# RWKV-7 attention and a GELU MLP on one core: the state turned in 64x64 tiles, fewer columns in the last chunk, and a new order of steps

## The chip, the cores and the metric

The kernel runs on one core of a Trainium2 chip (trn2). The metric is the time of one execution in microseconds of the device. Before the change it is the median of three runs.

## What is computed

Two blocks follow each other. The first is the recurrence of RWKV-7 over 768 time steps, for 4 x 8 heads of 40 x 40 state. The second takes the 3072 rows of 320 numbers that come out, and applies an MLP with an exact GELU.

```python
batch, n_heads, seq, head_dim = (4, 8, 768, 40)
n_tokens, d_model, d_ff = (3072, 320, 2048)
...
for t in range(S):
    kt, vt, rt = (k[:, :, t], v[:, :, t], r[:, :, t])
    wt, at, bt = (w[:, :, t], a[:, :, t], b[:, :, t])
    y[:, :, t] = np.einsum('bhd,bhde->bhe', rt, state)
    Sa = np.einsum('bhde,bhe->bhd', state, at)
    state_decay = state * wt[:, :, None, :] - np.einsum('bhd,bhe->bhde', Sa, bt)
    state = state_decay + np.einsum('bhd,bhe->bhde', vt, kt)
...
x = np.ascontiguousarray(attn_out.transpose(0, 2, 1, 3)).reshape(B * S, H * D)
h = x @ w_in
g = 0.5 * h * (1.0 + erf(h * inv_sqrt2))
return (g @ w_out).astype(np.float32)
```

Note that the state after the last time step is returned to nobody.

## The kernel before

**Chunks.** Time is cut into 12 chunks of C = 64 steps. Inside a chunk the recurrence is solved with matrix products: four products between the 64 steps (N, A, RV and the read of the old state), the inverse of a triangular matrix per head, and sums with the values. From chunk to chunk only the state goes on. All 32 heads are worked on together, two batches (e) by two (g), eight heads as four pairs (i) by two (x). A tile of partitions holds 64 rows of one half and 64 of the other, so most products are small: 40 or 64 rows by 64 columns, and matmuls on the four quadrants of the array follow each other. One fp32 matmul stands as two instructions in the trace.

**Combined columns.** VC = 104 columns are moved together where it goes: the first D = 40 belong to the next state, the other C = 64 to the outputs of this chunk. VR holds v beside the masked product RV, SM the solved right sides, st the state (40) beside the product of r with the state (64).

**The steps of a chunk c, and where they stand.** They are generators under `@step`; each `yield` ends one piece.

- `N` (t["nT"], t["aT"] to N): product on PE, mask on DVE, two stores to DRAM. `nb` loads that back with another layout, `inv` solves it on POOL in four pieces and stores it, `ft` loads the inverse into Tt. `corner` (L922 the transpose on DVE, then PE, then a copy on ACT to Js, L930) and `joined` (PE, and copies on ACT and DVE, L945) complete it.
- `A` and `RV` (masks at L692), `av` (A times VR, into PSUM), `X` (adds a times the state; two copies on ACT to SM at L957), `sa` (Tt times SM; two masks on DVE, L981).
- `tn` turns the state: a product with the identity on PE, and a copy on ACT into `turned` (L993). `yy` reads it: r times the state, into the 64 right columns of st (L1017).
- `QY` and `qk` (by_rows) sum SM and VR with b and k into PSUM; in the last chunk they move only the right 64 columns already. Then `state` makes the new state (L1098 to L1101) and `y` the outputs (L1048, L1049), which SP moves into xt.
- The MLP of the chunk: `ph` is the first matrix (chunks below 3 whole, L1175; from 3 on a scheme with seven products per half, L1200 and L1207, with copies `pc` on ACT at L1238, additions `pd` on DVE at L1244 and GELUs `pg` on ACT at L1250), `po` the second (L1272, then seven products at L1288), `tx` sums of x on DVE. Between ph's fifth and sixth product a copy (pc) and an addition (pd) read what the sixth goes on adding to.
- `co` and `ci` turn the weights, which arrive as pairs of words, into floats on DVE and ACT (L472 to L488). `warm` is a dummy product of 512 columns into a PSUM buffer that nobody reads.

Small steps load and scale: `a`, `b`, `k`, `v`, `r`, `w`, `wq`, `vp`, `bp`, `kp` issue loads on SP; `ta`, `tb`, `tk`, `tv`, `tr`, `wt` turn them on DVE (L577); `sk` (L621) scales on POOL; `sums` are the decay sums on PE with an Exp on ACT.

**The order** is written out by hand as one long list, ORDER. Each token takes a step one `yield` on, so the list is the program order of all five engines and of SP's queue, and each engine runs its own part of it in that order, waiting where data or a buffer isn't ready. Numbers behind colons name buffers: one of four PSUM buffers `duo0` to `duo3`, each two banks wide, or one of three `conv` tiles in SBUF. PSUM is only these four buffers, so a step must also wait until its buffer's last reader is done.

```python
for token in ORDER.split():
    name, *at = token.strip("*").split(":")
    places[:] = [int(x) for x in at]
    if name not in going:
        kind = name.rstrip("0123456789")
        going[name] = steps[kind](int(name[len(kind):]))
    next(going[name], None)
```

Constants of this case: NT = NB = NW = 3 and NS = 2 are the chunks up to which loads, turns and products have their first form, NP = 4 pairs of heads, G = 2, BW = 80, TW = 640. A matmul is recorded at L154 (`mm`), except those of ph, po and the transposes.

Of the kernel before, what the change touches and what calls it, by code (L numbers as in the profile page):

```python
# [35 lines left out]
sa0:0 sa0 sa0:1 tk1 warm3:2 wi0 wo0 inv1 sa0 tr1:0 QY0:1:2 wi0 qk0 ci9:0 logs2 tv1 ci3:1 ci9 tr1 ci9 y0 wl0 wl0 inv1
b2 state0 co0:0 sums2:0 co1:2 ci3 ci3 a2 wi1 sums2:3 sums2 r2 tn1:1 r2 wi1 wi1 sc2 A1:2 A1 co0 y0:3 ci4:1 tables0
sums2 y0:0 y0 y0 RV1:2 wi1 wi1 RV1 ci4 inv1 tn1 tr2:0 tr2 ta2:1 co0 co1 tb2:2 ta2 av1:0:3 tb2 zeros8 yy1:1 wo2 yy1 ci4
ci6:0 yy1 ci6 k2 ci7:1 inv1 co1 inv2 wi1 v2 ci6 ci8:2 ph0:2 X1 N2:1 sk2 X1 ph0 ft1 N2 ci8 corner1:0 X1 ph0 ph0:0
corner1:3 ci8 ph0 ci7 wo4 ft1 zeros6 tk2:2 zeros7 corner1 co3:0 co3 co5:2 co5 co3 wo9 zeros5 ft1 ci7 tv2:3 co2:0 N2 N2  # L40
a3 a3 joined1:1 ph0 ph0:0 wo8 co2 ph0 co9:1 tv2 co2 co4:0 joined1 joined1 co4 co9 co4 nb2 co9 tk2 co5 sa1:1:3 RV2:2
wo6 w3 inv2 sa1 nb2 ph0 ph0:0 ph0 co8:2 kp3 ph0 co6:1 sa1 w3 co7:0 wq3 co7 wo15 wq3 QY1:3:1 kp3 RV2 ta3 bp3 qk1 po0:2
po0 wo13 co6 co6 y1 bp3 co7 wt3:1 A2:0 state1 po0 y1 y1 y1 wt3 vp3 tn2:1 A2 av2:0:3 tn2 co8 logs3 wt3 wo10 yy2:1 yy2
vp3 vp3 po0 y1 co8 yy2 b3 co13:2 wt3 tb3 sums3:1 sums3 X2 wo12 ph1:1 co11:1 a4 co10:0 co10 co11 co11 vp3 X2 wo14 ta3
# [53 lines left out]
def kernel(  # L98
# [1300 lines left out]
```

## Time and profile before

| what | value |
|---|---|
| median of three runs | 658.70 us (658.08 to 658.98) |
| profiled execution | 657.67 us |
| its span, first to last instruction | 656.0 us |
| mean granted TensorE clock | 0.995 |
| moved by DMA | 80.73 MB, mean 123 GB/s |

The profiled execution is one run of its own, so a sum of parts is made against 657.67 us and its span, and the median is what a change is measured by. A row of the timeline gives start and length in us, engine, line, operation, what is written and read with buffer numbers left out, the shape and the number of instructions that were merged, and in brackets the idle time ahead with what ended it. Matmuls overlap at their ends, so the time of a step on TensorE is read from its start to the start of the next one.

### The profile page before, as it was taken

Reading aid. Unit: us, or ns where it says so; the run is one execution under the profiler, and the core shown is the slowest. Engines: PE = TensorE matmul, PEld = TensorE weight load, DVE = VectorE, ACT = ScalarE, POOL = GpSimd, SP = SyncE. Lnnn points to the kernel's source line nnn. Section 1 sums busy time; section 2 is a strip of 40 time slices with the busy share of each in tenths; the row PEclk is TensorE's granted clock in tenths of the full one; section 3 lists DMA queues with packets and bytes.
Section 4 is the critical chain, followed back from the end, with each engine's and each line's share of the span. In section 5 each row is a group of like instructions: output and inputs, shape, how many; then the busy total and the mean of one; then the engine's idle time right before and its main releaser. Section 6 shows DMA issues by size and latency. Waiting matters only on the chain.

```text
span 656.0 us, 30927 instructions
## 1 busy us (share of the span) xinstructions
PE 636.9 (97%) x13840; PEld 578.9 (88%) x13840; DVE 479.1 (73%) x643; ACT 272.4 (42%) x326; POOL 384.7 (59%) x797
## 2 busy tenths in 40 slices
PE   9998899999999999999999999999999999999987
PEld 5986788778788999999989999999999998999987
DVE  1698999998756986877886968967869854727332
ACT  4366362642253335337245346335346344134130
POOL 5258708826868838818848828848838848800000
PEclk9999999999999999999999999999999998999989
DMA  9989999687676585975696686775886673230100
GB/s 130 168 164 189 189 209 173 147 138 144 128 135 131 102 160 102 154 140 109 131 155 121 123 152 123 122 137 115 160 143 120 131 118 63 53 66 16 39 2 20
DMA packets 298949, 80.73 MB, mean 123 GB/s; under 512 B 287656, under 2 KB 292400, under 8 KB 298816
## 3 DMA queue, kind: packets, MB, share of 16 engines
q1 hardware_dynamic: 297952, 76.40, 63.3%
q0 software_dynamic: 864, 2.36, 2.3%
q8 instruction: 108, 1.77, 1.2%
q14 instruction: 25, 0.20, 0.1%
HBM read 65.40 MB, written 11.01 MB: 116 GB/s over the span
## 4 chain that ended last, share of the span: by engine, by line
PE 58%; DVE 14%; SPq 9%; DMA 7%; POOL 5%; issue 4%; ACT 2%; DVEq 0%; POOLq 0%; ACTq 0%
PE duo L1288 18%; PE duo L154 15%; PE duo L1200 15%; SPq L222 9%; PE duo L1207 4%; PE duo L1175 3%; PE duo L1272 3%; POOL os L817 2%; POOL rows L815 2%; DVE st L1101 1%; DMA Tt<-inv 1%; DVE xt L1049 1%; DVE conv L577 1%; DVE xt L1048 1%; DMA r_pairs<-in_r_dram 1%
## 5 line engine op out<-in xcount | busy, mean ns | idle before, releaser
L815 POOL TENSOR_TENSOR tmp<-W,Nb 128x56 f32<-128x56 f32 (+22 forms) x155 | 75.7, 489 | 48.0 <-DMA Nb<-N 36.2
L815 POOL TENSOR_TENSOR tmp<-rT,Nb 128x56 f32<-128x56 f32 (+22 forms) x155 | 73.1, 471 | 43.7 <-DMA Nb<-N 32.0
L1288 PE MATMUL duo<-w_out_sb,gt 128*128 128x160 f32 x640 | 92.5, 302 | 0.2 <-DVE gt L1314 0.2
L1288 PEld LDWEIGHTS duo<-w_out_sb,gt 128*128 128x128 f32 x640 | 87.7, 190 | 2.2 <-issue 0.4
L817 POOL TENSOR_TENSOR W<-W,tmp 128x56 f32<-128x56 f32 (+22 forms) x155 | 77.6, 500 | 12.2
L817 POOL TENSOR_TENSOR rT<-rT,tmp 128x56 f32<-128x56 f32 (+22 forms) x155 | 71.6, 462 | 12.2
L1200 PE MATMUL duo<-xt,w_in_sb 64*128 64x128 f32 x864 | 62.1, 276 | 0.0
L1238 ACT COPY gt<-duo 128x1024 f32<-128x1024 f32 x27 | 27.3, 1011 | 75.8 <-PE duo L1200 38.9
L1244 DVE TENSOR_TENSOR gt<-gt,duo 128x1024 f32<-128x1024 f32 x27 | 32.8, 1214 | 35.4 <-ACT gt L1238 18.0
L1207 PE MATMUL duo<-xt,w_in_sb 64*128 64x128 f32 x576 | 57.5, 276 | 0.0
L1200 PEld LDWEIGHTS duo<-xt,w_in_sb 64*128 64x128 f32 x864 | 54.2, 188 | 3.7 <-ACT SM L957 1.5
L1175 PE MATMUL duo<-xt,w_in_sb 64*128 64x256 f32 x480 | 54.8, 381 | 0.2 <-ACT w_tile L537 0.2
L1175 PEld LDWEIGHTS duo<-xt,w_in_sb 64*128 64x128 f32 x480 | 45.5, 187 | 5.9 <-ACT w_tile L537 0.4
L1288 PE MATMUL duo<-extra,conv 128*128 128x160 f32 x320 | 45.8, 301 | 1.0 <-DVE conv L1295 0.7
L1207 PEld LDWEIGHTS duo<-xt,w_in_sb 64*128 64x128 f32 x576 | 45.5, 192 | 0.0
L1288 PEld LDWEIGHTS duo<-extra,conv 128*128 128x128 f32 x320 | 43.8, 190 | 1.8 <-DVE conv L1295 0.9
L621 POOL TENSOR_TENSOR rows<-rows,w_tile 128x640 f32<-128x640 f32 x9 | 15.2, 1686 | 49.4 <-ACT w_tile L537 44.3
L957 ACT COPY SM<-duo 128x832 f32<-128x832 f32 x22 | 18.3, 852 | 47.6 <-PE duo L154 42.1
L1272 PE MATMUL duo<-w_out_sb,gt 128*128 128x320 f32 x128 | 36.9, 440 | 0.0
L1292 DVE TENSOR_TENSOR os<-os,duo 128x160 f32<-128x160 f32 x40 | 12.7, 317 | 31.4 <-PE duo L1288 27.2
L1250 ACT ACTIVATE gt<-gt 128x1024 f32<-128x1024 f32 x27 | 27.8, 1053 | 17.5 <-DVE gt L1244 17.4
L1272 PEld LDWEIGHTS duo<-w_out_sb,gt 128*128 128x128 f32 x128 | 23.6, 190 | 9.5
(257 smaller groups left out, 1421.6 us busy)
## 6 DMA issues: line engine op xcount, KB each, us to landing
Nb<-N SPq DMA_DIRECT2D x18, 256.0 KB
VR<-in_v_dram SPq DMA_DIRECT2D x24, 160.0 KB
out_dram<-os SPq DMA_DIRECT2D x48, 80.0 KB
rows<-in_b_dram SPq DMA_DIRECT2D x22, 160.0 KB
rows<-in_k_dram SPq DMA_DIRECT2D x22, 160.0 KB
w_out_sb<-in_moe_w_out_dram SPq DMA_DIRECT2D x5, 640.0 KB
w_tile<-in_w_dram SPq DMA_DIRECT2D x36, 80.0 KB
Tt<-inv SPq DMA_DIRECT2D x44, 64.0 KB
```

What stands on the lines that cost most here:

```text
L154: nc.tensor.matmul(o, lhsT, rhs, start=first, stop=True, skip_group_check=True)
L222: queue[0].dma_start(out=out, in_=in_)
L815: eng.tensor_tensor(t, W[:, :nr, j:j + 1].to_broadcast([P, nr, rest]), Nb[:, j:j + 1, j + 1:].to_broadcast([P, nr, rest]), ALU.mult)
L817: eng.tensor_tensor(W[:, :nr, j + 1:], W[:, :nr, j + 1:], t, ALU.add)
L1175: nc.tensor.matmul(pt[:, x, s], w_in_sb[half(x), kt, p * P:(p + 1) * P], xt[half(x), kt], start=kt == 0, stop=kt == NK - 1)
L1200: nc.tensor.matmul(out_of(pt)[:, x, j], left(kt, j)[half(x)], right[half(x), kt], start=first and j == 0 and kt == 0, stop=True, skip_grou ...
L1207: nc.tensor.matmul(out_of(pt)[:, x, j], w_in_sb[half(x), NP, at:at + P], xt[half(x), NP, cols], start=False, stop=True, skip_group_check=True)
L1238: nc.scalar.copy(block_of(f, g), out_of(of(c)["u"]))
L1244: nc.vector.tensor_tensor(block_of(f, g), block_of(f, g), out_of(of(c)[v_]), ALU.add)
L1250: nc.scalar.activation(block_of(f, g), block_of(f, g), ACT.Gelu)
L1272: nc.tensor.matmul(pt[:, g], gt[:, f, g * P:(g + 1) * P], w_out_sb[:, f], start=f == 0, stop=f == NF - 1)
L1288: nc.tensor.matmul(pt[:, n, :DM // 2], l_[:, f], r_[:, f], start=f == 0, stop=f == NF // 2 - 1)
```

## The change

Three things change. First, `tn` keeps its form for chunks 1 and 2, and from chunk 3 (NB) on it takes the two halves of the rows apart: 32 products of 40 rows and 40 columns on the four quadrants of the array, in place of 16 products of 128 rows and 80 columns; the copy reads PSUM in another pattern. Second, `wanted(c)` is the right 64 columns in the last chunk, and all 104 before; `av`, `X` with its copies and `sa` with its masks use it. So v of the last chunk is loaded but read by nobody. Third, ORDER is another one. It has the same 1553 tokens. Up to the second chunk's QY it is nearly the old sequence, with PSUM buffers 0 and 2 exchanged in the first lines; behind that the tokens stand in another sequence, with other buffers. Among them `warm7` moves from between `corner3` and `joined3` to behind `yy1`, and `warm4` from ahead of `corner7` to between the fifth and the sixth product of `ph11`.

The diff, with ORDER cut to the lines that hold the places the prediction speaks of:

```diff
@@ -29,68 +29,68 @@
...
-r4 po1 ft3 corner3:2 ph2:0 ph2 ft3 corner3:1 ft3 ph2 ww0 tr4 a5 warm7:3 a5 ws3 vp5 vp5 vp5 inv4 vp5 corner3 joined3:0
...
-sums7 sc7 pc6 ph6 po5 inv7 kp8 pc6 N8 ph6:3 ph6 wt9:2 N8 pd6 pg6 ft7 tk8:0 po5:1 ft7 warm4:0 corner7:0 nb8 corner7:0
-pc6 po5 pd6 A8:1 nb8 A8 corner7 ft7 joined7:0 joined7 joined7 ph6 a9 r8 r8 r8 sk7 w8 sa7:0:1 pg6 inv8 r8 ta9 inv8 w8
...
-nb9 nb9 tx7 tx7 inv10 ph7 ph7:1 pc7 ph7 po6:3 ft8 wt10:2 ft8 a10 wt10 pd7 sk8 r9 w9 corner8:0 wt10 pc7 r9 corner8:0
-po6 pd7 A9:3 corner8 inv9 joined8:0 joined8 joined8 inv9 ph7 A9 pd7 sa8:3:0 tx7 pg7 ph7 sa8 r9 pg7 pg7 a10 pg7 vp10
...
-N10:3 po7 a11 a11 sums9:1 y8 N10 tk10:2 inv9 ph8:0 pc8 ph8:3 tx8 ph8 inv9 ph8:2 po7 inv9 inv9 pc8 vp10 tv10 ph8 sums9
-tx8 N10 pd8 N10 ft9 corner9:2 ft9 ta11 nb10 nb10 ft9 po7:1 corner9:3 pg8 pc8 wq11 po7 sc9 pd8 A10:1 A10 wq11 bp11 sk9
...
-QY11:0:1 qk11 pg10 pg10 pd10 y11 y11 y11 pg10 po9 po10:0 pg10 po10:3 y11 po10 y11 po10:2 y11 po10 po10 po10:1 po10
-po10 y11 po10 po10 po10:3 po10 po10 y11 tx11 po10 po10:1 ph11:3 ph11:0 po10 po10 tx11 pc11 tx11 ph11 pc11 pd11 ph11:0
-ph11 pc11 pd11 ph11 pg11 tx11 tx11 ph11 pd11 pg11 pg11 pg11 po11:1 po11:0 po11 po11:2 po11 po11 po11:3 po11 po11 po11
...
+inv3 warm7:0 wo2 tails1 yy1 ci4 ci6:0 yy1 ci6 k2 ci7:1 inv1 co1 inv2 wi1 v2 ci6 ci8:2 ph0:0 X1 N2:2 sk2 X1 ph0 wo8 ft1
...
+ph6:3 po5 N8 wt9 tx6 ph6 ft7 sc7 corner7:0 ft7 corner7:2 tk8:0 ft7 nb8 po5 po5:1 nb8 corner7 joined7:2 joined7 po5
+ph6:1 a9 r8 pc6 pd6 joined7 ta9 pg6 sa7:2:3 sa7 sk7 sa7 ph6 pc6 pd6 QY7:2:3 tx6 tx6 r8 r8 qk7 state7 ph6 pd6 pg6 ph6
...
+sums8 a10 ph7:1 pc7 ph7:2 ph7 ph7:3 vp10 X8 pc7 pd7 corner8:0 corner8:2 corner8 ft8 ph7 A9:2 vp10 wt10 r9 r9 joined8:0
+tx7 sk8 pc7 pd7 A9 inv9 joined8 ph7 tx7 joined8 sa8:0:2 ta10 pd7 r9 r9 sc8 sa8 vp10 w9 sa8 vp10 w9 ph7 inv10 QY8:2:0
...
+X9 tx8 po7 a11 y8 N10 N10 N10 inv9 tv10 A10:2 wq11 tx8 sums9:3 po7 po7:0 sums9 po7 sc9 tx8 nb10 ph8:3 pc8 ph8:0 ta11
+pd8 X9 ph8 pc8 wq11 wt11:2 nb10 tx8 ph8:0 ph8 pc8 ft9 sk9 corner9:0 ft9 ft9 corner9:1 corner9 r10 joined9:1 joined9
+pg8 r10 pd8 ph8 A10 pg8 r10 joined9 tx8 pd8 sa9:1:2 w10 w10 wt11 ph8 bp11 r10 sa9 sa9 QY9:2:1 logs10 wt11 pg8 pg8 tr10
...
+y9 y9 po8:0 po8 y9 y9 sums10 kp11 tn10 sc10 k10 RV10 po8 av10:1:3 yy10:2 vp11 inv10 ta11 po8 po8 tb11 yy10 po8:0 po8
...
+QY11:1:0 k11 sk11 qk11 y11 y11 y11 y11 y11 po10 po10:2 po10 po10 y11 po10:0 po10 po10 tx11 po10 po10 tx11 tx11 po10:2
+po10 y11 po10 po10 po10:0 ph11:2 v11 y11 ph11:1 pc11 ph11 ph11:3 pd11 pc11 pg11 tx11 ph11 tx11 pc11 pd11 warm4:1 ph11
+pg11 ph11 pd11 po10 po10 pg11 po11:1 po11:0 pg11 po11 po11:2 po11 po11 po11:2 po11 po11 po11 po11 po11:0 po11 po11
...
@@ -770,8 +770,12 @@
             return
         t["av"] = [duo()[:, :, :NP * VC].rearrange("p g (i d) -> p g i d", i=NP) for x in range(2)]
         for g, i, x, e, q, m in units(True):
-            mm(t["av"][x][half(e ^ x), g, i], t["A"][half(e), x, g, i], VRs[c % 2][half(e), g, q, m], i == 0)
-        yield
+            mm(t["av"][x][half(e ^ x), g, i, wanted(c)], t["A"][half(e), x, g, i], VRs[c % 2][half(e), g, q, m, wanted(c)],
+               i == 0)
+        yield
+
+    def wanted(c):
+        return slice(D if c == NCH - 1 else 0, VC)
 
     sm_of = SM.rearrange("p g q (a x) c -> p x g (q a) c", x=2)
 
@@ -951,10 +955,11 @@
     def X(c):
         t = of(c)
         for g, i, x, e, q, m in units():
-            mm(t["av"][x][half(e ^ x), g, i], t["aT"][half(x, D), g, i, e], st[half(x, D), e, i, g], False)
+            mm(t["av"][x][half(e ^ x), g, i, wanted(c)], t["aT"][half(x, D), g, i, e], st[half(x, D), e, i, g, wanted(c)],
+               False)
         yield
         for x in range(2):
-            nc.scalar.copy(sm_of[:, x], t["av"][x])
+            nc.scalar.copy(sm_of[:, x, :, :, wanted(c)], t["av"][x][:, :, :, wanted(c)])
             yield
 
     @step
@@ -975,22 +980,33 @@
             return
         pt = [duo()[:, :, :NP * VC].rearrange("p g (i d) -> p g i d", i=NP) for x in range(2)]
         for g, i, x, e, q, m in units():
-            mm(pt[x][half(e), g, i], Tt_tile[half(e ^ x), x, g, i], sm_of[half(e ^ x), x, g, i])
+            mm(pt[x][half(e), g, i, wanted(c)], Tt_tile[half(e ^ x), x, g, i], sm_of[half(e ^ x), x, g, i, wanted(c)])
         yield
         for x in range(2):
-            nc.vector.tensor_tensor(sm_of[:, x], pt[x], left_upper.unsqueeze(1).unsqueeze(1).to_broadcast([P, G, NP, VC]),
-                                    ALU.mult)
+            mask = left_upper.unsqueeze(1).unsqueeze(1).to_broadcast([P, G, NP, VC])[:, :, :, wanted(c)]
+            nc.vector.tensor_tensor(sm_of[:, x, :, :, wanted(c)], pt[x][:, :, :, wanted(c)], mask, ALU.mult)
             yield
 
     @step
     def tn(c):
-        pt = duo()[:, :, :NP * BW].rearrange("p e (n t) -> p e n t", n=NP)
+        if c < NB:
+            pt = duo()[:, :, :NP * BW].rearrange("p e (n t) -> p e n t", n=NP)
+            for e in range(2):
+                for i in range(NP):
+                    for g in range(G):
+                        mm(pt[half(g), e, i], st[:, e, i, g, :HP], ident.rearrange("p (x d) -> p x d", x=2)[:, :, :D])
+            yield
+            nc.scalar.copy(turned[:, :TW].rearrange("p (e n) -> p e n", e=2), pt.rearrange("p e n t -> p e (n t)"))
+            yield
+            return
+        pt = duo()[:, :, :G * NP * D].rearrange("p x (n d) -> p x n d", d=D)
         for e in range(2):
             for i in range(NP):
                 for g in range(G):
-                    mm(pt[half(g), e, i], st[:, e, i, g, :HP], ident.rearrange("p (x d) -> p x d", x=2)[:, :, :D])
-        yield
-        nc.scalar.copy(turned[:, :TW].rearrange("p (e n) -> p e n", e=2), pt.rearrange("p e n t -> p e (n t)"))
+                    for x in range(2):
+                        mm(pt[half(g), x, e * NP + i], st[half(x, D), e, i, g, :HP], ident[half(x, D), half(x, D)])
+        yield
+        nc.scalar.copy(turned[:, :TW].rearrange("p (n x d) -> p x n d", x=2, d=D), pt)
         yield
 
     def sums_of_y(c):
```

More of the change, by code (lines that the diff above doesn't have):

```diff
@@ L41 @@
[L41 to L44, printed above, removed]
-co13 ph1 ph1 ph1:0 co10 ph1 inv2 ph1 ph1:1 tv3 co13 co14:0 co15:2 a4 co14 inv2 inv2 k3 inv2 co15 co12:1 ph1 X2 co14
@@ L94 @@
+joined11:0 sums11 sc11 ph10 tx10 joined11 ph10 pd10 po9 joined11 sa11:0:1 pg10 sa11 sa11 pg10 pg10 po10:0 pg10 po10:2
+QY11:1:0 k11 sk11 qk11 y11 y11 y11 y11 y11 po10 po10:2 po10 po10 y11 po10:0 po10 po10 tx11 po10 po10 tx11 tx11 po10:2
+po10 y11 po10 po10 po10:0 ph11:2 v11 y11 ph11:1 pc11 ph11 ph11:3 pd11 pc11 pg11 tx11 ph11 tx11 pc11 pd11 warm4:1 ph11
+pg11 ph11 pd11 po10 po10 pg11 po11:1 po11:0 pg11 po11 po11:2 po11 po11 po11:2 po11 po11 po11 po11 po11:0 po11 po11
+po11 po11:2 po11 po11
 """
```

95 lines of the change are left out of this document (48 added, 47 removed).

## The prediction

> **What bounds the kernel now.** I read the page first, then the busy time by stage, then the waits, then the timeline. The page gives the shares.
>
> ```profile
> span 656.0 us, 30927 instructions
> ...
> PE 636.9 (97%) x13840; PEld 578.9 (88%) x13840; DVE 479.1 (73%) x643; ACT 272.4 (42%) x326; POOL 384.7 (59%) x797
> ```
>
> TensorE is busy for 97% of the span. A share is a mean over stages, so the stages come next (start:end, length, then busy time of PE, PEld, DVE, ACT, POOL, granted clock, DMA share, GB/s).
>
> ```profile
> 72.00:148.00 76.00, 73.23 (x1439) 60.49 (x1438) 72.68 (x126) 36.47 (x48) 40.33 (x86) 1.00 0.85 170
> 148.00:240.00 92.00, 91.48 (x1883) 77.65 (x1874) 70.26 (x81) 33.92 (x40) 66.28 (x135) 1.00 0.70 132
> 240.00:540.00 300.00, 297.77 (x7069) 283.34 (x7069) 233.14 (x281) 133.21 (x151) 204.69 (x410) 1.00 0.73 131
> 540.00:656.00 116.00, 107.40 (x1972) 103.94 (x1964) 52.68 (x76) 31.80 (x39) 30.93 (x64) 0.97 0.19 38
> ```
>
> From 148 to 540 us TensorE idles 0.5 + 2.2 us of 392, so an instruction taken from it there shortens the run, as long as no wait takes its place. Before 148 VectorE is as full (72.68 of 76). After 540 there are 8.6 idle us, and the clock falls to 0.97. The waits name the causes (total, times, longest).
>
> ```profile
> PE duo L154 <- issue: 4.5, 4, 1.7
> PE duo L1200 <- DVE gt L1244: 2.6, 2, 2.4
> ...
> PE duo L154 <- DVE conv L922: 0.7, 1, 0.7
> ...
> DVE conv L922 <- DMA Tt<-inv: 12.6, 5, 5.3
> ```
>
> The 2.4 us wait is ph's sixth product, which stands behind an addition on VectorE. In the last row VectorE waits for the inverse that came back through memory, five times: that chain arrives just in time, though TensorE pays only 0.7 us for it yet (the row above).
>
> **The change part by part.** *The turned state.* tn has 16 matmuls of 128 rows, 64 weight columns and 80 moving columns, which the trace records as 32 instructions. From chunk 3 on it is 32 matmuls of 40 rows and 40 moving columns, 64 instructions, nine times. The new form is in no row, so it is bounded by its neighbours. The timeline of chunk 11 (start, length):
>
> ```profile
> 569.80 1.33 PE L154 MATMUL duo<-ident,st 128*64 128x80 f32 x32
> 571.05 1.66 PE L154 MATMUL duo<-VR,nT 64*64 64x104 f32 x64
> 572.53 1.11 PE L154 MATMUL duo<-rT,turned 40*64 40x64 f32 x64
> 573.57 2.44 PE L1288 MATMUL duo<-extra,gt 128*128 128x160 f32 x16
> 575.94 1.66 PE L154 MATMUL duo<-st,aT 40*64 40x104 f32 x64
> 577.53 2.50 PE L1200 MATMUL duo<-xt,w_in_sb 64*128 64x128 f32 x40
> ...
> 593.77 1.66 PE L154 MATMUL duo<-SM,Tt 64*64 64x104 f32 x64
> 595.35 0.71 PE L1200 MATMUL duo<-xt,w_in_sb 64*128 64x128 f32 x8
> ...
> 598.23 1.16 PE L154 MATMUL duo<-SM,rows 64*64 64x64 f32 x64
> 599.22 1.11 PE L154 MATMUL duo<-VR,rows 64*64 64x64 f32 x64
> 600.26 4.61 PE L1288 MATMUL duo<-w_out_sb,gt 128*128 128x160 f32 x32
> ```
>
> A step costs what lies between its start and the next start. tn costs 571.05 - 569.80 = 1.25 us. yy, 64 instructions on the same 40x64 tiles with 64 moving columns, costs 573.57 - 572.53 = 1.04. Below that stand steps of small tiles in chunk 7. A form of 64x64 tiles of which two run at a time tells whether columns still count.
>
> ```profile
> 394.84 0.75 PE L154 MATMUL duo<-conv,spare 32*32 32x32 f32 x64
> 395.52 1.16 PE L154 MATMUL duo<-aT,kT 40*64 40x64 f32 x64
> 396.61 0.75 PE L154 MATMUL duo<-Tt,Js 32*32 32x32 f32 x64
> 397.29 0.49 PE L1200 MATMUL duo<-xt,rows 64*128 64x128 f32 x4
> ```
>
> And by form (count | busy us, mean ns | idle before):
>
> ```profile
> L154 PE MATMUL duo<-w_in_sb,Nb 64*64 64x64 f32 x64 | 2.2, 221 | 0.0
> L154 PE MATMUL duo<-w_in_sb,Nb 64*64 64x32 f32 x64 | 2.0, 218 | 0.0
> ```
>
> 64 instructions of 32x32 tiles take 0.68 us (395.52 - 394.84), the low end; yy's 1.04 is the high end. In the last two rows halving the columns takes only 0.2 of 2.2 us, so loading 64 weight columns is the floor there, not moving 64. I take 0.93, near yy and a little below, because 40 columns move instead of 64 and because tn now has the tile shape of av behind it in most chunks. Saved: 9 x (1.25 - 0.93) = 2.9 us; ends 9 x 0.21 = 1.9 and 9 x 0.57 = 5.1. The copy out of PSUM keeps 128 x 640 elements. It lies beside av (1.48 us by the rows above) and costs nothing as long as it takes less; what it takes beyond, yy would wait for, nine times.
>
> [...]
>
> *The last chunk.* av, X and sa move 64 of 104 columns. They cost 1.48 (572.53 - 571.05), 1.59 (577.53 - 575.94) and 1.58 us (595.35 - 593.77). QY and qk of this chunk already have the 64 columns, and cost 0.99 (599.22 - 598.23) and 1.04 (600.26 - 599.22). With 1.02 each the three save 1.6 us; ends 1.5 and 1.7. Two copies on ACT and two masks on DVE shrink too, off TensorE's path. v's load for chunk 11 now has no reader and moves behind y11's loads on SP; only two output stores are queued behind it, which wait for later products anyway. k11's load moves on SP behind the store that follows the product of 573.57, still over 20 us ahead of qk11 (599.22), which hides it; were it later than that, POOL's scaling and qk11 would wait for it one to one.
>
> *The order: a filler in the last gap.* One dummy matmul, warm4, moves from 393.89 us to the gap ahead of ph11's sixth product. The timeline, and the chain that ended last:
>
> ```profile
> 393.89 1.02 PE L154 MATMUL duo<-cum_m,ident 128*128 128x512 f32 x2
> ...
> 629.02 0.80 PE L1200 MATMUL duo<-xt,rows 64*128 64x128 f32 x4 [2.37 <-DVE gt L1244]
> ```
>
> ```profile
> 626.70 1.02 ACT gt L1238
> ...
> 627.75 1.23 DVE gt L1244
> ```
>
> And the busy times in windows of 3.41 us, the length in which the clock changes here:
>
> ```profile
> 55.59:59.00 3.41, 1.75 (x79) 1.55 (x75) 1.44 (x3) 1.51 (x2) 2.86 (x7) 1.00 1.14 221
> 59.00:62.42 3.42, 2.61 (x77) 1.87 (x77) 3.38 (x6) 0.73 (x1) 3.10 (x5) 1.00 0.83 112
> 540.29:543.70 3.41, 1.74 (x139) 1.43 (x130) 3.09 (x3) 1.24 (x3) 2.85 (x8) 1.00 0.30 47
> 543.70:547.11 3.41, 3.41 (x33) 3.41 (x34) 0.69 (x1) 2.98 (x4) 2.79 (x8) 0.50 0.32 55
> 625.60:629.02 3.42, 1.06 (x20) 0.86 (x16) 1.27 (x2) 1.98 (x3) 0.00 (x0) 1.00 0.02 5
> 629.02:632.43 3.41, 3.40 (x32) 3.41 (x34) 0.49 (x2) 1.04 (x1) 0.00 (x0) 0.50 0.00 0
> ```
>
> The chain copy, addition, sixth product keeps its 2.37 us. But 1.0 us of work (394.84 - 393.89 = 0.95) goes into it that stood on the full stretch at 394. And behind a window of 3.42 us that was busy for 1.06 the clock stands at 0.50 for 3.41 us, which costs half of that, 1.7. A window busy for 1.74 was followed once by 0.50 (543.70) and once, at 1.75, by 1.00 (59.00): the edge lies there. With the filler the last gap's window is busy for about 2.1, so I expect the full clock: saved 1.0 + 1.7 = 2.7; ends 1.0 and 2.7.
>
> [...]
>
> A second dummy, warm7, moves from chunk 3 to ahead of 148 us, where TensorE still idles 2.8 us (76 - 73.2). That takes 1.0 us from the full stretch; I enter 0, since ahead of 148 it delays what is queued behind it; ends -1.0 and 0.
>
> *The order: the rest.* Up to the second chunk's QY only few steps move; behind it the steps stand in another sequence, and the four PSUM buffers are dealt anew. I added up the paces of PE steps between each producer and its reader. Two places are shorter than what the rows ask: between ph's fifth and sixth product 2.37 us of copy and addition must fit. Chunk 7 now has A and joined there (1.09 + 0.68 from the rows at 395.52 and 396.61), chunk 8 corner and joined (0.68 + 0.68). That adds 0.6 and 1.0 us of waiting, 1.6 in all, where before both chunks had more between. The remaining hand-overs come out as in the old order, between tn and the state ahead of it even wider; I enter them at 0, with 3 us to both sides, the size of the small waits that the old order has after 148 us (0.5 + 2.2).
>
> *The sum*, against the profiled execution of 657.67 us (span 656.0 and 1.7 around it): -2.9 - 1.6 - 2.7 + 1.6 = -5.6, so 652.1. The profiled execution is 1.0 us below the median of 658.70, so beside that median I forecast 653.1.
>
> **The rivals.** *The inverse comes late: slower.* Between N(c) and corner(c) lie a mask, a store, a load, the inverse on POOL, a store and a load. In chunk 10:
>
> ```profile
> 476.43 1.11 PE L154 MATMUL duo<-aT,nT 40*64 40x64 f32 x64
> ...
> 535.24 0.71 DVE L922 STREAM_TRANSPOSE conv<-Tt 128x512 f32<-128x512 f32 x1 [1.73 <-DMA Tt<-inv]
> ...
> 540.34 0.74 PE L154 MATMUL duo<-conv,N 32*32 32x32 f32 x63
> ```
>
> The chain takes 535.95 - 477.54 = 58.4 us, and its DVE step waited 1.73 for the transfer, so it can't be much shorter. corner10 came 62.8 us after N10. In the new order X9 comes in between (+1.6), the last product of chunk 8's output (-2.4, as at 573.57) and A11 (-1.1) go out, tn is shorter (-0.3): 60.6, so 2.2 us of slack are left where 4.4 were. Chunk 7 comes out about as tight. Nor are the loads' places on SP the same: in chunks 7 and 10 an output store, which waits for VectorE, is queued ahead of the load that POOL waits for. Each us beyond the slack is a us of TensorE, and a wait near 1.7 brings a half-clock window of 1.7 more. From 5.6 us in all the change is lost. Three chunks late by 2 us with two such windows are 9.4: 662.5. For it: five waits on that transfer before. Against it: they made TensorE wait only once, 0.7 us.
>
> *Hand-overs eat the gain: no change.* VectorE is full until 148, and its order there changes: a mask of chunk 1 now waits for sa1, and the weight conversions that the second half of po0 reads come right before it. If such waits, and those behind ph's fifth product, sum to 5 us more than my 1.6, the time is 658.
>
> *More is gained.* The stall at 541 (idle 3.41 - 1.74 = 1.67 us, then 1.7 us of half clock) belongs to "issue", a wait that nothing in the profile explains. If it falls away with the new order, another 3.4 us go: 649.7.
>
> *The new tn doesn't run four at a time.* Then it costs what the two-at-a-time row shows, 2.0 us instead of 1.25: 9 x 0.75 = 6.8 more instead of 2.9 less, 662.8. Against it: X, with the same four tiles in turn, moves 104 columns in 1.59 us for 64 instructions, four at a time. 3%.
>
> **How the numbers follow.** Forecast (650.5 to 656) 0.55; more is gained (below 650.5) 0.13; hand-overs eat the gain (656 to 660) 0.16; the inverse late, 0.13, and tn not in parallel, 0.03, both above 660. The range 648.5 to 659.5 leaves out the last two and the lower edge of the second. A measurement of this kernel tells about 0.2%, 1.3 us, from no change: faster than 657.4 are the first two and a little of the third, 0.73; within it 0.10; slower 0.17.
>
> **What would show it.** Right: 64 instructions with 40 columns that take about 0.93 us in the timeline, 64-column rows for av, X and sa in the last chunk, a granted clock of 1.00 behind the last gap, waits of 0.6 and 1.0 us on the addition in chunks 7 and 8, and hardly less idle time elsewhere. Wrong: TensorE waiting on the transpose ahead of corner by over 1 us, a second half-clock window, or a tn of more than 1.1 us.

## The result, and the profile after

The changed kernel takes 665.3 us (median of six executions, 660.2 to 669.2) beside 658.8 us of the kernel before on the same chip (six executions): a ratio of 1.0104, with a 95% interval of 1.0069 to 1.0139. It is slower by about 6.5 us where I forecast 5.6 less. Measured a second time (h0 below), the ratio was 1.0065 (1.0036 to 1.0095). The profiled execution of the changed kernel, 669.2 us, is the slowest of the first six, so its trace shows more loss than the median has.

From the page of the changed kernel: span, busy time of the engines, and the queue that carries instructions (packets, MB, share of 16 engines).

```profile
span 667.5 us, 31520 instructions
...
PE 639.5 (96%) x14128; PEld 580.0 (87%) x14128; DVE 488.1 (73%) x643; ACT 272.8 (41%) x326; POOL 386.0 (58%) x797
...
q8 instruction: 111, 1.82, 1.2%
```

TensorE has 288 matmul records more than before (14128 - 13840): nine turns with 32 more each. The instructions come in blocks: 1.82 MB in 111 packets are 16.4 KB each. The kernel before has 108 of them:

```profile
q8 instruction: 108, 1.77, 1.2%
```

Each matmul record has its weight load (PEld x14128 and x13840), so if these packets carry TensorE's instructions alone, one holds 28256 / 111 = 255 of them, and 27680 / 108 = 256 before.

The busy time by stage, in the windows of the prediction:

```profile
72.00:148.00 76.00, 70.06 (x1361) 57.80 (x1361) 66.48 (x112) 38.13 (x50) 37.01 (x84) 0.96 0.78 152
148.00:240.00 92.00, 90.79 (x1931) 75.73 (x1928) 69.79 (x80) 32.12 (x39) 61.93 (x127) 1.00 0.75 130
240.00:540.00 300.00, 290.51 (x6947) 276.27 (x6946) 239.07 (x283) 130.22 (x146) 208.12 (x407) 0.99 0.72 129
540.00:667.50 127.50, 121.08 (x2382) 116.00 (x2380) 62.40 (x89) 35.52 (x43) 35.85 (x76) 1.00 0.26 50
```

Before, TensorE was idle for 2.2 us of the 300 from 240 to 540; now it is idle for 9.5. From 72 to 148 it is idle for 5.9 instead of 2.8, and there VectorE, which was nearly full, now idles 9.5 us; for 4.8 of them it waits for TensorE. The waits of TensorE (total, times, longest):

```profile
PE duo L154 <- issue: 10.4, 8, 2.5
PE duo L154 <- DVE conv L926: 2.5, 2, 2.3
...
PE duo L1216 <- DVE gt L1260: 1.5, 2, 1.3
PE duo L1216 <- DVE os L1308: 1.2, 1, 1.2
```

"issue" has grown from 4.5 to 11.0 us (10.4 here and 0.6 at another line), the wait for the inverse (conv, L926) from 0.7 to 2.5, and the wait for the addition (gt) has shrunk from 2.6 to 1.5. The changed steps themselves became shorter, about as forecast. The timeline of chunk 5's turn, and the last chunk's av by form (count, busy us, mean ns, idle before):

```profile
276.39 1.14 PE L154 MATMUL duo<-ident,st 40*64 40x40 f32 x64
277.34 1.64 PE L154 MATMUL duo<-VR,nT 64*64 64x104 f32 x64
```

```profile
L154 PE MATMUL duo<-VR,nT 64*64 64x64 f32 x64 | 1.2, 221 | 0.0
```

From one start to the next the new turn costs 277.34 - 276.39 = 0.95 us (old: 1.25); over the nine new turns it is 0.91 to 1.32, and 0.95 in the middle.

To see where the time went I took, for every step of TensorE, the distance to the next step's start, less the same step's usual distance (its median over the chunks), and added that up by stage. The third column is a second profiled execution of the changed kernel (h0, span 663.8).

| stage, us | before | after | after, again |
|---|---|---|---|
| 71 to 110 | 0.9 | 7.7 | 0.2 |
| 110 to 133 | 0.8 | 2.1 | 4.8 |
| 133 to 300 | 0.4 | 1.1 | 0.8 |
| 300 to 400 | 1.3 | 8.7 | 8.8 |
| 400 to 500 | 1.1 | 0.8 | 0.4 |
| 500 to 550 | 3.6 | 4.6 | 3.4 |
| 550 to the end | 3.0 | 1.9 | 1.8 |
| sum | 11.1 | 26.9 | 20.2 |

The changed steps save 4.6 at these distances (turn and columns). Lost are 15.8 more in one execution and 9.1 in the other, where another 3.2 had been lost ahead of the table's start: 11.2 and 7.7 in all, beside spans that are 11.5 and 7.8 longer. The early 7.7 came once and not again; the 300-to-400 stage, chunks 6 and 7, came twice.

### The profile page after: what moved, and what is told of

Read it like the earlier page. It is cut to its first block, busy times and chain, and to the rows that moved or that the text cites. A ratio compares the mean times of both kernels' runs of the same rounds, so it can differ in the third digit from the quotient of the medians.

```text
span 667.5 us, 31520 instructions
## 1 busy us (share of the span) xinstructions
PE 639.5 (96%) x14128; PEld 580.0 (87%) x14128; DVE 488.1 (73%) x643; ACT 272.8 (41%) x326; POOL 386.0 (58%) x797
## 3 DMA queue, kind: packets, MB, share of 16 engines
q8 instruction: 111, 1.82, 1.2%
## 5 line engine op out<-in xcount | busy, mean ns | idle before, releaser
L819 POOL TENSOR_TENSOR tmp<-W,Nb 128x56 f32<-128x56 f32 (+22 forms) x155 | 73.0, 471 | 62.6 <-DMA Nb<-N 50.8
L819 POOL TENSOR_TENSOR tmp<-rT,Nb 128x56 f32<-128x56 f32 (+22 forms) x155 | 75.7, 488 | 57.7 <-DMA Nb<-N 45.9
L1304 PE MATMUL duo<-w_out_sb,gt 128*128 128x160 f32 x640 | 94.2, 305 | 0.3 <-DVE os L1308 0.2
L1304 PEld LDWEIGHTS duo<-w_out_sb,gt 128*128 128x128 f32 x640 | 89.3, 193 | 3.0 <-DVE os L1308 0.6
L821 POOL TENSOR_TENSOR rT<-rT,tmp 128x56 f32<-128x56 f32 (+22 forms) x155 | 73.6, 475 | 12.2
L1191 PE MATMUL duo<-xt,w_in_sb 64*128 64x256 f32 x480 | 58.6, 398 | 0.9 <-issue 0.6
L1216 PEld LDWEIGHTS duo<-xt,w_in_sb 64*128 64x128 f32 x864 | 54.2, 188 | 4.3 <-DVE os L1308 1.4
L1191 PEld LDWEIGHTS duo<-xt,w_in_sb 64*128 64x128 f32 x480 | 48.0, 197 | 8.7 <-issue 1.8
L1223 PEld LDWEIGHTS duo<-xt,w_in_sb 64*128 64x128 f32 x576 | 44.8, 190 | 0.7 <-DVE xt L1182 0.4
L1288 PEld LDWEIGHTS duo<-w_out_sb,gt 128*128 128x128 f32 x128 | 23.7, 190 | 9.9 <-issue 0.3
L962 ACT COPY SM<-duo 128x832 f32<-128x832 f32 (+1 forms) x22 | 17.8, 827 | 32.8 <-PE duo L154 32.8
```

Of the source, the lines that this page charges most:

```text
L819: eng.tensor_tensor(t, W[:, :nr, j:j + 1].to_broadcast([P, nr, rest]), Nb[:, j:j + 1, j + 1:].to_broadcast([P, nr, rest]), ALU.mult)
L821: eng.tensor_tensor(W[:, :nr, j + 1:], W[:, :nr, j + 1:], t, ALU.add)
L1191: nc.tensor.matmul(pt[:, x, s], w_in_sb[half(x), kt, p * P:(p + 1) * P], xt[half(x), kt], start=kt == 0, stop=kt == NK - 1)
L1216: nc.tensor.matmul(out_of(pt)[:, x, j], left(kt, j)[half(x)], right[half(x), kt], start=first and j == 0 and kt == 0, stop=True, skip_grou ...
L1223: nc.tensor.matmul(out_of(pt)[:, x, j], w_in_sb[half(x), NP, at:at + P], xt[half(x), NP, cols], start=False, stop=True, skip_group_check=True)
L1288: nc.tensor.matmul(pt[:, g], gt[:, f, g * P:(g + 1) * P], w_out_sb[:, f], start=f == 0, stop=f == NF - 1)
```

## The experiments

Theory, formed from these two traces: "issue" is TensorE waiting for its own instructions. In it they arrive in blocks of 256, as the packets above give them (load and matmul, so 128 matmul records; one fp32 product is two records, as the turn's 32 products stand as x64). Counted by matmul records, the kernel before waits on "issue" at 1239, 1620, 4556 and 11959, the changed one at 1239, 1620, 1876, 2131, 3790, 6342, 7108, 7491 and 12213: all of them, but for a slow drift, on multiples of 128 plus the same number. In the kernel before a chunk has about 1148 records, 9 x 128 - 4, so each chunk's block ends fall into nearly the same steps. The new turn and the new sequence put other steps there. Rivals: the waits belong to hand-overs of the new order (VectorE, the inverse), or the new turn itself is slow.

All ratios are to the kernel before, measured beside each of them, with 95% intervals; its medians were 658.8 to 660.3 us.

| kernel | median us | ratio |
|---|---|---|
| changed kernel | 665.3 | 1.0104 (1.0069 to 1.0139) |
| e1: changed code, order of before | 670.8 | 1.0172 (1.0129 to 1.0214) |
| e2: changed order, old turn | 664.5 | 1.0092 (1.0057 to 1.0128) |
| e3: changed, ends moved by 62 records | 679.1 | 1.0306 (1.0260 to 1.0351) |
| e4: before, ends moved by 62 records | 684.3 | 1.0383 (1.0347 to 1.0419) |
| f1: before, ends moved by 128 records | 664.2 | 1.0074 (1.0048 to 1.0099) |
| f2: before, with columns and filler | 655.5 | 0.9951 (0.9925 to 0.9976) |
| f3: e1 with 16 products in the turn | 657.9 | 0.9967 (0.9936 to 0.9997) |
| g1: before, with columns | 659.7 | 0.9994 (0.9969 to 1.0019) |
| g2: before, with filler | 658.0 | 0.9973 (0.9949 to 0.9998) |
| g3: f2, ends moved by 8 records | 658.3 | 0.9987 (0.9955 to 1.0018) |
| h0: changed kernel again | 663.5 | 1.0065 (1.0036 to 1.0095) |
| h1: h0, loads spread | 663.0 | 1.0051 (1.0019 to 1.0084) |
| h2: h1, chunk 9's inverse earlier | 663.3 | 1.0058 (1.0027 to 1.0089) |

**One part alone: e1 and e2.** e1 is the changed kernel with ORDER taken back, e2 the changed kernel with tn taken back.

```diff
 ORDER, e1:
-N1 sq0:3 sq1:0 sq0 sq1 sq1 tv0:1 sk0 tk0:2 sq0 sq0 sq1 sq0:0 tk0 sq0 N1 zeros0 sq0 N1 sq0 sq1:3 tv0 A0:2 sq1 wi0 sq1
+N1 sq0:3 sq1:2 sq0 sq1 sq1 tv0:1 sk0 tk0:0 sq0 sq0 sq1 sq0:2 tk0 sq0 N1 zeros0 sq0 N1 sq0 sq1:3 tv0 A0:0 sq1 wi0 sq1
...
 tn, e2, in all chunks:
...
-mm(pt[half(g), x, e * NP + i], st[half(x, D), e, i, g, :HP], ident[half(x, D), half(x, D)])
+mm(pt[half(g), e, i], st[:, e, i, g, :HP], ident.rearrange("p (x d) -> p x d", x=2)[:, :, :D])
```

> The changed tn, av, X and sa in the order of before: one part of the change alone. Theory (the order and the fetch of TensorE's instructions lose the time, not the new code): the code saves about 9 x 0.3 us in tn and 1.5 us in the last chunk, so about 654.5 us; TensorE's stream has 576 instructions more, so its 256-instruction blocks end elsewhere and up to 4 us can come or go with that. Rival (the new tn costs more than it saves): 660 us or more. Rival (the inverse chain is what became late): no wait of TensorE on the transpose ahead of corner here, and about 654.5.

> The new order and the 64 columns of the last chunk, but tn in its old form in all chunks. Theory (the order loses it): still 663 to 669 us, with waits called issue of over 6 us in sum. Rival (the new tn loses it): back to 659 or less.

Both are slower than the kernel before, and e1, where only cheaper steps were put in, is the slower one; the first number that I expected of it, 654.5, is missed by 16 us. That speaks against a sum of step times, and against a slow turn too: seven of e1's nine new turns take 0.95 to 1.08 us, and the other two take less than in the kernel before. The copy behind the turn takes 0.69 us in both forms. Two of the largest waits in the timeline of e1 stand inside the joining product (Tt, Js) of chunks 8 and 9, where the kernel before had none:

```profile
450.21 0.31 PE L154 MATMUL duo<-Tt,Js 32*32 32x32 f32 x11 [1.53 <-issue]
...
501.10 0.75 PE L154 MATMUL duo<-Tt,Js 32*32 32x32 f32 x38 [2.92 <-issue]
```

Both rows begin in the middle of a step of 64 records: no producer of data is waited for there. The end of a block drifts through the steps, as a chunk has 32 records more. e1's profiled execution (664.6 us, the fastest of its six) is 7.0 us longer than that of the kernel before. The work itself is 2.9 us shorter (the forecast has 4.5 for turn and columns), but "issue" is 7.0 us longer and the half clock, counted as half of TensorE's busy time under it, costs 2.8 more (in the changed kernel the same two rows of ph start 0.43 us apart under it, from 510.33, and 0.23 at the full clock, from 642.96). The joining product of chunk 9 alone takes 2.9 us of wait and 2.7 of half clock.

In e2 the waits on "issue" are twice those of f2 (below), which has the same steps in the order of before. The waits of e2, then of f2:

```profile
PE duo L154 <- issue: 8.6, 9, 2.2
```

```profile
PE duo L154 <- issue: 4.2, 4, 1.7
```

**The block ends moved and nothing else: e3, e4, f1.** One dummy product near the start (warm6) is cut into 32 small ones, 62 records more, in the changed kernel (e3) and the kernel before (e4); f1 cuts it into 65, which is 128 records, one whole block.

```diff
 def warm(c):
-    mm(duo()[:, 0], ident, cum_m.unsqueeze(1).to_broadcast([P, 4, P]))
+    pt = duo()
+    if c == 6:
+        for n in range(32):   # f1: 65
+            j, x = n // 2 % 2, n % 2
+            mm(pt[half(j), x, :HP], ident[half(x), :HP], cum_m[half(x), :HP])
+    else:
+        mm(pt[:, 0], ident, cum_m.unsqueeze(1).to_broadcast([P, 4, P]))
```

> The changed kernel, with one early dummy product (warm6) cut into 32 small ones of the same total length, which nobody reads: 124 instructions more ahead of everything that follows, so that each 256-instruction block of TensorE's stream ends 62 matmuls earlier in the work. Theory (fetch of instructions): the waits called issue at 78, 93, 196 and 338 us go or come at other steps, their positions in the stream keep their distance of a multiple of 128 matmuls, and the time moves by over 2 us either way. Rival (waits for data or buffers, such as the inverse chain): the same steps wait for the same time and the median stays within 1.5 us of the changed kernel's 665.

> The kernel before with the same cut of warm6 into 32 small products, nothing else. Theory (fetch of instructions): its stalls at 59, 77 and 542 us go or come at other steps, and the time, 658.8, moves by over 2 us either way. Rival (waits for data): the stalls stay at the same steps and the time within 1.5 us of 658.8.

> The kernel before with warm6 cut into 65 small products instead of 32: the stream gets 256 instructions, one whole block, in front, so every block ends at the same step as in the kernel before. Theory (place of the block ends): back at 658 to 661 us, with the stalls of the kernel before and none ahead of joined. Rival (the cut products as such, or the longer stream, cost the time): 684 us or more, as with 32 of them.

Half a block makes the changed kernel 2% slower than it was and the kernel before 3.8%, 25 us for 31 small products more at the start. The waits and the timeline of e4:

```profile
PE duo L154 <- issue: 18.9, 11, 2.9
```

```profile
311.82 0.19 PE L154 MATMUL duo<-Tt,Js 32*32 32x32 f32 x1
314.11 0.38 PE L154 MATMUL duo<-Tt,Js 32*32 32x32 f32 x21 [2.09 <-issue]
```

That wait comes in every chunk from 4 to 9, ahead of or inside the joining product, about 1148 records apart. With a whole block more (f1), so with twice as many small products, those waits are gone and the later ones stand in the same steps as in the kernel before. Its timeline, and that of the kernel before:

```profile
550.82 0.41 PE L154 MATMUL duo<-aT,kT 40*64 40x64 f32 x16
551.16 0.74 PE L154 MATMUL duo<-conv,N 32*32 32x32 f32 x63
553.09 0.21 PE L154 MATMUL duo<-conv,N 32*32 32x32 f32 x1 [1.19 <-issue]
```

```profile
540.82 0.26 PE L154 MATMUL duo<-conv,N 32*32 32x32 f32 x9
542.28 0.21 PE L154 MATMUL duo<-conv,N 32*32 32x32 f32 x1 [1.21 <-issue]
```

The same 64th product of the same step waits for the same time. f1 is still 0.7% slower, where I had expected 658 to 661. Its profiled execution is 10.1 us longer than that of the kernel before, and 8.7 of them are lost ahead of 84 us: 3.4 in one wait at 22 and 3.2 to the half clock beside it.

**The block by itself: f4.** Behind the kernel before stand 512 small products (1024 records) each with 64, 128 and 256 columns. Only the last output stores, in the first 3 us, run beside them (in the trace of the kernel before the packets of the last one end at 654.3, 2.6 us behind TensorE's last product); past them the program issues no transfer.

```diff
+def dense(c):
+    pt = duo()
+    for n in (1, 2, 4):
+        for k_ in range(512):
+            j, x = k_ // 2 % 2, k_ % 2
+            right = cum_m[half(x), :HP * n] if n < 4 else cum_m[half(x)].unsqueeze(1).to_broadcast([HP, 2, P])
+            mm(pt[half(j), x, :HP * n], ident[half(x), :HP], right)
```

> The kernel before with three runs of 512 small products behind its last one, on the four quadrants, with 64, 128 and 256 columns; nothing reads them. No transfer runs there. A block of 256 instructions is 128 matmul records: about 1.9, 3.4 and 6.8 us of work. Theory (a block can't follow the one before it sooner than its fetch takes, about 3.3 us): in the first run a wait called issue every 128 records, 1 to 2 us each; in the second 0 to 0.5; in the third none. Rival (fetches are late only under the load of other transfers): no such wait.

The timeline of f4:

```profile
652.71 2.10 PE L155 MATMUL duo<-cum_m,ident 64*64 64x64 f32 x128 [1.55 <-issue]
656.46 2.10 PE L155 MATMUL duo<-cum_m,ident 64*64 64x64 f32 x128 [1.65 <-issue]
660.20 2.10 PE L155 MATMUL duo<-cum_m,ident 64*64 64x64 f32 x128 [1.65 <-issue]
663.67 2.09 PE L155 MATMUL duo<-cum_m,ident 64*64 64x64 f32 x128 [1.38 <-issue]
```

A wait stands behind every 128 records, and the rows are 3.5 to 3.75 us apart, though 128 such records run in 2.1. Here TensorE got no more than 256 instructions in 3.5 us, where my theory had 3.3. With 128 columns, where 128 records run in 3.6 us (17.92 for 640), two waits of 0.3 us are left, with 256 none. So in this run a block cost TensorE up to 1.65 us where its work was dense, and nothing with 256 columns. The 128 records between two waits, with a load to each, are the 256 instructions that the packets give too (255 and 256).

**The new turn with no instruction more: f3.** e1 with 16 products per turn, of 64x64 tiles; half of the state's rows are left out.

```diff
 def tn(c):   # from chunk 3
+    for e in range(2):
+        mm(pt[half(g), e, i], st[half(e, D), e, i, g, :HP],
+           ident[half(e, D)].rearrange("p (x d) -> p x d", x=2)[:, :, :D])
```

> The changed kernel in the order of before, with tn from chunk 3 on in 64x64 tiles but only 16 products of 40 rows and 80 columns, as many as the old tn: half of the state's rows are left out of the turned state. Theory (the number of instructions moved the block ends): the ends are where they were before, tn costs about 0.6 instead of 1.25 us, so 658.8 - 5.9 - 1.5 = 651 to 653 us. Rival (the tiles or their copy cost the time): 664 or more, as with 32 products in this order.

The time goes from 670.8 (e1) to 657.9: the waits stand at the steps of the kernel before again. That is what the theory asks of it. But I had expected 651 to 653. Five of the nine turns take 0.60 to 0.70 us; those of chunks 6, 7, 9 and 10 take 1.07 to 1.76 from their start to the next step's. In all four VectorE is still making the state when the turn begins. The step behind the turn then waits 0.6 us for a copy on ScalarE in chunk 6 and 0.4 us for a mask on VectorE in chunks 7 and 10. In chunks 6 and 9 the kernel before takes 1.76 and 1.84 as well. So the saving on the turn is partly given back to the engines beside it.

**Columns and filler: f2, g1, g2, g3.** The order of before with the old turn, 64 columns in the last chunk (g1), warm4 moved into the last gap (g2), both (f2), both with warm6 cut into five, 8 records (g3).

```diff
-... tk8:0 po5:1 ft7 warm4:0 corner7:0 nb8 corner7:0
+... tk8:0 po5:1 ft7 corner7:0 nb8 corner7:0
-ph11 pc11 pd11 ph11 pg11 tx11 ...
+ph11 pc11 pd11 warm4:1 ph11 pg11 tx11 ...
```

> The order of before with the old tn, the 64 columns of av, X and sa in the last chunk, and warm4 moved into the last gap of ph: the two parts of the change that leave the number of TensorE's instructions per chunk as it was. Theory: -1.5 for the columns and -2.7 for the filler (1.0 of work and 1.7 of half clock), so 654.6 us. Rival (those parts bring nothing, or the filler's window stays slow): 657 to 659.

> The kernel before with 64 of 104 columns of av, X and sa in the last chunk, the filler left where it was. The work saved is 1.6 us, and no product is added or dropped ahead of the last chunk, so the ends of TensorE's blocks of instructions stay where they were. Theory (instruction blocks): 657.3, i.e. 1.6 below the kernel before, ratio 0.9975. If a saved product is worth nothing here: 658.9.

> The kernel before with the one dummy product warm4 moved from chunk 7 into the gap ahead of the last ph product. By the working of the forecast -2.7 (1.0 of work, 1.7 of half clock): 656.2, ratio 0.9959. [...] With the columns kernel the two should add up to the kernel that has both (655.5, -3.4).

> Columns and filler together, and one dummy product (warm6) near the start cut into five, which puts every later block end 8 records (16 instructions) earlier in the program, without a whole block more. Theory (instruction blocks): a few records are enough to move an end into or out of a step, so 655.5 with 2 us to both sides. If the place of the block ends doesn't matter: 655.5 within 0.5.

f2 is faster than the kernel before by 0.24 to 0.75% (3.2 us), and so faster than the changed kernel too. The windows of f2 around the last gap:

```profile
625.13:628.54 3.41, 2.10 (x23) 1.15 (x19) 1.27 (x2) 1.99 (x3) 0.00 (x0) 1.00 0.00 0
628.54:631.95 3.41, 3.41 (x60) 3.41 (x62) 0.90 (x3) 1.03 (x1) 0.00 (x0) 1.00 0.00 0
```

The first window is busy for 2.10 us and the second keeps the full clock, as forecast. In all nine traces with the filler there the clock behind the last gap stays full. With the gap left open it falls to half in four traces (before, e1, f3, g1), and not in three (e4, f1, f4): so the 1.7 us of half clock are lost in some executions only. g1's interval (-2.0 to +1.3 us) holds the 1.6 of the forecast and nothing at all; it doesn't tell them apart. g2's (-3.4 to -0.1) holds both ends of the forecast for the filler, 1.0 and 2.7. g3's overlaps f2's, so 8 records can't be told from none.

**The changed order's own places: h0, h1, h2.** Two kinds of late instructions show in the traces. In both, TensorE resumes 2.2 to 3.3 us after the start of an instruction packet. In the dense kind that packet starts up to 1.9 us behind the previous block end. In the other kind it starts 2.1 to 6.7 us behind it, mostly while the DMA engines are full. In the changed kernel X of chunk 6 is of the other kind. Timeline, then the DMA queues from 329.80, close behind that block's start, to 335.20 and from there to 337.80 (packets, MB, share of the window):

```profile
334.19 1.07 PE L154 MATMUL duo<-st,aT 40*64 40x104 f32 x38
337.72 0.78 PE L154 MATMUL duo<-st,aT 40*64 40x104 f32 x25 [2.47 <-issue]
```

```profile
q1 hardware_dynamic: 4792, 0.98, 108.8%
```

```profile
q1 hardware_dynamic: 1542, 0.33, 99.6%
q8 instruction: 1, 0.02, 2.6%
```

For 5.4 us the loads take all that the queues have, and no instruction packet starts; the one that TensorE needs starts at 335.3. The second place is corner of chunk 9, whose load stands on SP behind loads for later chunks, although GpSimd had issued the inverse's store by 493.7. SP's timeline:

```profile
499.18 1.11 SPq L222 DMA_DIRECT2D v_pairs<-in_w_dram  x2
500.33 0.50 SPq L222 DMA_DIRECT2D Nb<-N  x1
500.94 5.13 SPq L222 DMA_DIRECT2D Tt<-inv  x6
```

```profile
507.56 0.75 PE L154 MATMUL duo<-conv,spare 32*32 32x32 f32 x64 [2.28 <-DVE conv L926]
508.79 0.75 PE L154 MATMUL duo<-Tt,Js 32*32 32x32 f32 x64 [0.47 <-ACT Js L934]
```

```diff
-tv7 po4:0 po4 wq8 inv6 inv6 ta7 wq8 b6 inv6 ... X6 sums6:0 a8 kp7 N7 ... X6 y5 inv6 po4       (h1, h2)
+tv7 kp7 po4:0 po4 wq8 inv6 inv6 ta7 wq8 inv6 ... X6 sums6:0 N7 ... X6 y5 inv6 b6 a8 po4
-wq11 wt11:2 nb10 tx8 ph8:0 ph8 pc8 ft9 sk9 corner9:0 ft9 ft9                                  (h2)
+ft9 nb10 tx8 ph8:0 ph8 pc8 sk9 corner9:0 wq11 wt11:2 ft9 ft9
```

> The changed kernel once more, for the spread of its stalls from one execution to the next. Three places that the changed kernel and the kernel with its order and the old turn share: TensorE idle ahead of X of chunk 6 (near 337 us), at corner of chunk 9 (near 507) and at the turn of chunk 2 (near 125). Theory (they belong to the order): all three are there again, 2.5, 2.3 and 1.1 us within 1. Theory (chance of one execution): at least one is gone. The time: 665 within 3.

> The changed kernel, with three of the seven loads that stand together ahead of X of chunk 6 moved (the second half of k, both of b and a). Theory (a block of TensorE's instructions is fetched late, because its packet is queued behind a burst of loads): the fetch of that block starts within 2.5 us of the block end instead of 5.8, the idle time of 2.5 us at X of chunk 6 goes with the half clock behind it (1.7), and the time falls by about 4 to 661. Theory (only where the block ends counts): the block end is still in X, so idle time and time stay, 665.

> As the kernel with the spread loads, and on SP the first load of chunk 9's inverse ahead of two loads for chunks 10 and 11 (w's second half and one of N's blocks). Theory (the inverse comes late in chunk 9 since its load is queued behind them): the load is issued 2 us earlier, corner of chunk 9 waits 0.4 instead of 2.3 us, the half clock behind it goes too, and the time falls by another 3 to 4, to 657 to 658. Theory (GpSimd's inverse itself is the late one): no change against the kernel with the spread loads.

In h0 the three places are there again, two of them with other sizes; its timeline:

```profile
335.59 0.79 PE L154 MATMUL duo<-st,aT 40*64 40x104 f32 x10 [2.47 <-issue]
...
503.80 0.75 PE L154 MATMUL duo<-conv,spare 32*32 32x32 f32 x64 [0.90 <-DVE conv L926]
```

The third, at the turn of chunk 2, is there with 1.8 us instead of 1.1. In h1 the wait at X falls, but not away (first row, h1):

```profile
334.40 0.78 PE L154 MATMUL duo<-st,aT 40*64 40x104 f32 x25 [0.95 <-issue]
```

The packet starts 4.3 us late instead of 5.8, once the loads that were left (w, 480 KB) have drained. So moving loads alone seems to shorten the wait, at the same block end (one execution; e2, with the loads unmoved, waits 1.77 there); my 2.5 us was too bold. In h2, with the same loads moved, X waits 1.33 us, and 6.8 us at half clock stand there as in h0. The second place, corner of chunk 9, waits for nothing in h2, but other waits stand close by (h2):

```profile
509.83 0.56 PE L154 MATMUL duo<-Tt,Js 32*32 32x32 f32 x6 [0.71 <-ACT Js L934]
...
522.54 0.77 PE L154 MATMUL duo<-w_tile,cum_m 64*64 64x320 f32 x8 [1.18 <-ACT gt L1268]
```

Neither moves the time clear of noise: h1 and h2 lie within 0.15% of h0, where I had expected 4 and 7 us less. The intervals would hide some 3 us. So the two places are real, but they are not shown to carry the loss.

## Why the prediction was wrong

**The bound** was right: TensorE is the bound, and what it loses goes into the time one to one (11.2 and 7.7 us more lost, spans 11.5 and 7.8 us longer). But I took the wait named "issue" for one that nothing in the profile explains. The page has the row that does, the queue of instructions; its packets, read by window as above, show each of these waits behind a block end.

**The turn** was sized right: 0.95 us beside my 0.93, so 2.7 us of work are saved. It is not 2.7 us of time. The same step brings 64 instructions per chunk in place of 32 in the trace's count, and with the order of before that costs 1.8% (e1, 1.0172, beside g1, 0.9994), about 11 us, where I had -2.9. In the changed order the turn is worth nothing that can be measured: 1.0104 with it and 1.0092 without (e2), with intervals that overlap. With f3, which saves more work and adds no instruction, the loss is gone. That the number of instructions and not the form of the turn does it is what e1, f3 and e4 show together; e1 with its block ends shifted back was not tried.

**The last chunk's columns** run in the time that I gave them; the 1.6 us are within g1's interval, which also holds 0. **The filler** did what its step says: 2.10 us busy in the last gap's window, full clock behind it, 1.31 us left of the gap. Both together brought 3.2 us (1.6 to 4.9) in f2 beside my 4.3. That warm7 moves for nothing was not tried by itself. **The new waits on the addition** in chunks 7 and 8, 1.6 us in my sum, did not come: the two waits on gt that are left are the last gap (1.3) and 0.2.

**The step that failed** is the last one: "the remaining hand-overs come out as in the old order ... I enter them at 0, with 3 us to both sides". The changed order with the old turn is 0.9% slower than the kernel before (e2), and 1.4% slower than f2, which differs from it in the order alone: some 9 us. I had counted producers and readers of data, and the bounds were the size of the old order's small waits. Part of what I left out has no producer in the program: each 128 matmul records TensorE needs a block, which came late where the step there was dense (waits of 1.38 to 1.65 us in f4) or the DMA queues were full (2.47 us at X of chunk 6, share 108.8%). The other part is the half clock, which I had priced at the last gap, at the stall at 541 and for a late inverse only. Added up over the traces of e2 and f2, whose spans are 664.9 and 653.9: "issue" 8.6 and 4.2 us, all other waits above 0.15 us 8.1 and 8.3, half clock 5.1 and none (each trace's last few us left out). So in these two executions 9.5 of the 11.0 us are "issue" and half clock, and waiting for data has not grown. Still, of e2's three slow stretches only one stands behind a wait on "issue" (X of chunk 6); the other two stand behind waits for VectorE (the turn of chunk 2) and for the inverse (chunk 9). The windows of the changed kernel show how a wait and the clock add up.

```profile
76.16:79.57 3.41, 1.41 (x42) 0.97 (x41) 1.81 (x4) 1.12 (x3) 0.77 (x4) 1.00 0.72 104
...
335.57:338.98 3.41, 1.26 (x34) 0.85 (x33) 3.14 (x5) 0.92 (x1) 2.71 (x10) 1.00 0.92 127
338.98:342.39 3.41, 3.41 (x18) 3.33 (x15) 0.00 (x0) 3.38 (x5) 2.27 (x5) 0.57 0.58 98
506.30:509.71 3.41, 1.68 (x132) 1.53 (x134) 2.91 (x3) 0.54 (x3) 2.72 (x9) 1.00 0.52 105
509.71:513.12 3.41, 3.41 (x40) 3.41 (x39) 1.02 (x3) 3.38 (x4) 2.80 (x8) 0.56 0.56 100
```

The clock of 0.57 and 0.56 is a mean: it is 0.50 for 3.41 us from 339.5 and from 510.1. So each of the two idle stretches costs its own 1.7 to 2.5 us and then 1.7 more, half of 3.41.

**The rivals.** The inverse came late once, in chunk 9 and not in 7 and 10, by 2.3 us in one execution and 0.9 in another; I had priced three chunks. Hand-overs that eat the gain came too: the turn of chunk 2 waits 1.1 and 1.8 us for the state on VectorE, and one product of ph, near 248 us, waits 1.2 us in both executions for VectorE's additions to os. The stall at 541 did fall away, as the rival with more gain had it, and others came in its place.

**Open.** The sums above are of one execution each; how the 9 us of the order split by place in the program is not settled. The stage from 300 to 400 us loses 7.4 us more than before in both traces of the changed kernel, and 5.0 and 6.4 us of it are waits at block ends in the steps A and X (3.3 and 3.0) with the half clock behind them (1.7 and 3.3); but when h1 took most of the wait at X away, the time stayed. I also formed a first theory in which the drift of the ends explains the changed kernel itself. For e1 it holds. For the changed kernel it does not go far: 9.0 of its 11.0 us of "issue" are of the kind with a late packet, not of the dense kind (6.1 of 7.9 in h0).

## What to carry to other kernels

Where TensorE runs many short instructions (128 records in 2.1 us in f4) and its waits are put down to "issue", count its instructions in blocks, here of 256, and look which steps stand at the ends; a change that adds or drops some shifts all ends behind it, and a neutral shift of half a block (2% and 3.8% here, e3 and e4) is a cheap test of how much a measured gain or loss is due to that. Price an instruction that is added not only by its own time. And take the independent pieces of a change alone: here two of four were worth 3 us, and the other two lost more.

## What the hardware showed that I had not expected

- Blocks of 256 instructions of TensorE followed each other no faster than every 3.5 to 3.75 us, even with no transfer of the program beside them (f4).
- At the same wait on "issue" near 60 us, six kernels that are alike up to that point waited 0.55, 1.2, 1.7, 1.7, 2.5 and 3.2 us (g1, g2, before, f2, f3, e1). The DMA queues are full there (share 0.9 to 1.1). That may be part of why single executions of one kernel differ by some us.
- Inside the spans of before and after the half clock (0.50) stands for 3.41 us at a time, six times: from 543.69 and 629.02 before, from 80.06, 93.71, 339.47 and 510.14 after. In the changed kernel a window of 3.41 with 1.45 us of idle time (busy 1.96, from 90.30) was followed by it, and so was one with 1.30 (busy 2.11, from 506.73). But the traces show no sharp edge. In the clock's own windows, counted in steps of 3.41 us from a change of the clock, one that was busy for 2.60 us was followed by the half clock (413.58 in e4), and ones busy for 1.40 (56.16 in the changed kernel), 1.66 (56.57 in h1) and 1.75 were not. The edge that the forecast read from two windows, near 1.75, is not borne out.
